# Linear attention and a gated FFN on one core: the first FFN product of two pairs of groups as seven half products, and numerators finished in PSUM

## The chip, the cores and the metric

The kernel runs on one core of a Trainium2 chip. The metric is device time in microseconds (us), from start to end of one execution; lower is better. Before the change three runs gave 367.69, 367.46 and 368.05 us, median 367.69. PE is the matrix engine, DVE the vector engine, ACT the scalar engine, POOL the GpSimd engine, SP the engine that issues most transfers. PE writes to PSUM, which has eight banks of 128 x 512 fp32; ACT and DVE read it.

## The reference

The inputs are q, k, v of (8 batches, 8 heads, 576 tokens, 64) and the weights. What is computed, cut from the reference:

```
def phi(x):
    proj = np.einsum('bhsd,df->bhsf', x, w_phi)
    proj = proj - np.max(np.abs(proj), axis=-1, keepdims=True)
    return np.concatenate([np.exp(proj), np.exp(-proj)], axis=-1)
q_p, k_p = (phi(q), phi(k))
kv = np.einsum('bhsf,bhsd->bhfd', k_p, v)
z = np.sum(k_p, axis=2)
num = np.einsum('bhsf,bhfd->bhsd', q_p, kv)
den = np.einsum('bhsf,bhf->bhs', q_p, z)[..., None] + 1e-06
...
x = (num / den).transpose(0, 2, 1, 3).reshape(4608, 512)
gate = np.maximum(x @ w_gate, 0.0)      # 512 -> 1536
val = x @ w_val                         # 512 -> 1536
return (gate * val @ w_out)             # 1536 -> 512
```

## The kernel before

**Units of work.** A batch has 512 tokens in four tiles of 128, and 64 left over. The leftovers of all eight batches make one more group of 512 tokens. So the FFN has nine groups: 0 to 7 for the batches and 8 for the leftovers (its steps carry the number of batches, 8; its tile is `xTm`, the others' are `xTs`). All of it is written as small steps, functions `do_xx`. The string `ORDER` lists some 2200 words such as `fv.3.7:5`, which is step `fv` for group 3, block 7, in PSUM bank 5; `@val2` gives a buffer. The words are recorded one after the other, and each engine does its own instructions in that order. So `ORDER` alone decides what an engine does next, in which bank and in which buffer. Groups run staggered: attention of batch b+1 lies between FFN steps of group b.

**Attention of one tile of 128 tokens.** `nu` (L904) multiplies the two feature halves (s = 0 and 1, from exp and exp of the negative) of a query tile `qp` with `kv`, for two or three heads in one bank, 65 columns for each head and s: 64 numerators and a denominator. Three `nu` cover eight heads. `nt` (L925) on DVE multiplies the s = 1 part with a scale `cq` into a buffer `t`; `nv` (L935) adds the s = 0 part into `u`; `nr` (L943) takes one reciprocal of eight denominators into `r`; and `nx` (L947) on POOL multiplies `u` with `r` into `xu` (bf16). `xt` transposes `xu` by DMA into `xT`, 512 features on partitions and 512 tokens along a row. `mn` (L1060) is `nu` for the leftover group.

**The FFN of a group.** For each of 12 blocks of 128 hidden features `fv` and `fg` (both through L1081) make `val` and `gate`: four matmuls of 128 x 128 weights on 512 tokens, one for each quarter of the 512 features. `va` (L1096, ACT) or `vb` (L1099, DVE) copies `val` to SBUF, and `ga` (L1102, DVE) makes `h = max(gate, 0) * val`. Group 0 does the same in quarter pieces (`pv`, `pg`, L1110).

**The second product** of groups 1 to 8 is already done with seven products of half size in place of eight: `fw` (L1247), each 12 matmuls of 256 columns. It needs four sums over halves of `h` for six blocks, `ps` on POOL or `ds` on DVE (both L1223), and sums of `w_out` made once, `tw` (L1203). Two of the sums write over `h` in place. The seven results are put together in SBUF: `ys` and `y2` copy on ACT (L1272, L1275), `yw`, `yz`, `y1`, `y3` and `y4` add on DVE (L1278). `ow` sends rows out.

**Filler.** `zz` (L442) multiplies zeros, 85 matmuls in the first part of the program.

Of the kernel before, what the change touches and what calls it, by code (L numbers as in the profile page):

```python
# [28 lines left out]
vd.0.0.0:2@vs1 qz.0.0:3@my1 vs.0.1.1 qe.0.1.1.1:5 vp.0:2 qu.0.1@mz0 ke.0.2.1.0:6 qe.0.1.1.0:5 wl.0.0
vz.0:2 qb.0.2:4 zz.2:7 qb.1.3:3 zz.2:7 qb.1.2:1 vd.0.0.1:2 qu.0.0@mz1 vz.1:2 qe.0.1.3.0:3@qp2  # L30
vo.2@vs2 qw.0.0@cq0 qx.0.0.3:0 qx.0.0.2:4 qe.0.0.0.0:2 vs.0.2.1 zz.7:7 kv.0.0:6 qx.0.1.3:3 lw.1.1
vs.0.2.0 kc.0.0:6@kv0 kt.1.1@kT3 qe.0.0.0.1:2 kv.0.2:5 kv.0.1:6 qe.0.0.2.1:4@qp3 lm.1.1 kc.0.2:5
wl.1.1 kc.0.1:6 nu.0.0.0:2 nt.0.0.0:2@t0 zz.1:7 nu.0.0.2:5 qw.0.1 qx.0.1.2:1 qe.0.0.2.0:4
qe.0.1.3.1:3 nu.0.0.1:6 nv.0.0.0:2@u0 zz.2:7 nu.0.1.2:4 lv.1.2 nu.0.1.0:2 qe.0.1.2.1:1 nt.0.0.1:6@t1
lm.1.0 nt.0.0.2:5@t2 qy.0.2:3 nv.0.0.1:6 qe.0.0.3.0:0 nv.0.0.2:5 nt.0.1.0:2@t3 zz.2:7 nu.0.1.1:6
qy.0.3:5 nr.0.0@r0 qe.0.1.2.0:1 qz.0.2:3@my2 nv.0.1.0:2@u1 qz.0.3:5@my0 qu.0.2@mz2 zz.5:7
kr.1.1:3125 qe.0.0.3.1:0 nt.0.1.2:4@t0 nt.0.1.1:6@t1 qw.0.2 wl.1.0 nu.0.2.2:0 nx.0.0@xu0 nv.0.1.2:4
xp.0.0:7 nv.0.1.1:6 nt.0.2.2:0@t2 ke.1.1.3.1:5@kp3 nr.0.1@r1 nu.0.2.1:4 xa.0.0:7 nt.0.2.1:4@t3
nu.0.2.0:6 ke.1.1.0.1:3 nt.0.2.0:6@t0 qu.0.3@mz1 ke.1.1.0.0:3 pv.1.0:7 nv.0.2.1:4@u2 nv.0.2.2:0
nv.0.2.0:6 nu.0.3.1:4 qw.0.3 ke.1.1.1.0:1 nx.0.1@xu1 kx.1.1.0:3@mk3 xp.0.1:0 pa.1.0:7@val0  # L40
# [12 lines left out]
qe.1.0.3.1:4 qe.1.0.2.1:7 vs.1.1.0 qx.1.0.3:4 qe.1.0.0.0:0 qe.1.0.0.1:0 fv.0.10:1 va.0.9:6@val0 wo.0
vq.1.0 kr.1.2:5046 vq.1.1 pb.0.3:2 qx.1.0.2:7 kx.1.2.0:5@mk5 qe.1.0.1.1:3 va.0.10:1@val3
qe.1.0.1.0:3 qe.1.0.2.0:7 kv.1.1:2 mt.0 wo.1 kx.1.2.3:6 qy.1.0:1 kc.1.1:2@kv1 fg.0.9:3
ke.1.2.0.0:5@kp0 qz.1.0:1@my1 kx.1.2.1:0 kx.1.2.2:4 ke.1.2.3.1:6 ku.2@kT3 vo.1.0@vs1 ke.1.2.1.1:0
kk.1.2.0@ek4 qu.1.0@mz0 vs.1.0.1 kk.1.2.1 ke.1.2.3.0:6 fv.0.8:7 ga.0.9:3 ke.1.2.0.1:5 fg.0.10:2
# [216 lines left out]
def kernel(  # L274
# [679 lines left out]
    def do_nx(bk, b, i):  # L954
        normalize(nc.gpsimd, b, i)
# [408 lines left out]
```

## Time and profile before

| | |
|---|---|
| median of the runs shown (lowest to highest) | 367.69 us (367.46 to 368.05) |
| the profiled execution: first to last instruction, which is the time that the profile gives for it | 365.2 us |
| difference between the two | 2.5 us |
| mean granted PE clock | 0.997 |
| matmuls, and weight loads | 3900 each |
| transfers: bytes, mean rate | 38.14 MB, 104 GB/s |

The profile is of one execution. Its page has the busy time of each engine as a share of the span, the chain of work that ended last, followed back from the end, and groups of instructions by source line with the mean time of one. A matmul's end is modelled, so that one of 512 columns is listed with 379 ns, though the next one starts sooner; how closely matmuls follow each other is read from pieces of the chain, which give a start, a length and a count. Windows give the busy time of each engine in a stretch of the span.

### The profile page before, as it was taken

The page shows a single profiled execution, that of the slowest core. Times are in us where ns is not written, and L with a number is a line of the kernel's source. Part 1 is how long each engine was busy: PE and PEld are TensorE (multiplying, and loading weights), DVE is VectorE, ACT ScalarE, POOL GpSimd, SP SyncE. Part 2 cuts the span into 40 slices and gives each one's busy share as a digit, 9 for nine tenths or more (in the row PEclk, how much of TensorE's full clock was granted, in tenths as well). Part 3 has the DMA queues.
Part 4 walks back from the last instruction along what each step waited for, and adds up shares of the span by engine and source line. Part 5 has one row for each costly group of instructions (what it writes and reads, how often), then busy time and mean ns, then how long its engine had stood idle before and what let it go on. Part 6 is the DMA issues. An engine that isn't in the chain of part 4 may idle for free.

```text
span 365.2 us, 10031 instructions
## 1 busy us (share of the span) xinstructions
PE 356.6 (98%) x3900; PEld 224.4 (61%) x3900; DVE 308.1 (84%) x723; ACT 228.8 (63%) x550; POOL 275.8 (76%) x337
## 2 busy tenths in 40 slices
PE   8999999999999999999999999999999999999993
PEld 6579865445575647755676456755457765545682
DVE  5999999989999998989988989899676945448872
ACT  4999996986698768695975278748854221121200
POOL 8765988999999999968997589946975793016600
PEclk9999999999999999999999999999999999999998
DMA  8999999983746893298219660397000320203016
GB/s 128 254 205 206 176 196 143 181 132 53 131 96 131 103 156 71 58 149 109 61 63 126 130 130 0 61 177 137 0 16 2 131 45 0 72 3 115 2 33 197
DMA packets 90768, 38.14 MB, mean 104 GB/s; under 512 B 64226, under 2 KB 86370, under 8 KB 90722
## 3 DMA queue, kind: packets, MB, share of 16 engines
q0 software_dynamic: 33504, 15.03, 32.5%
q1 hardware_dynamic: 56754, 21.83, 27.7%
q10 hardware_dynamic: 464, 0.66, 0.8%
q8 instruction: 30, 0.49, 0.6%
q14 instruction: 16, 0.13, 0.1%
HBM read 37.81 MB, written 9.44 MB: 129 GB/s over the span
## 4 chain that ended last, share of the span: by engine, by line
PE 81%; DVE 9%; POOL 4%; issue 2%; DMA 1%; ACT 1%; SPq 0%; DVEq 0%; POOLq 0%
PE bank L1081 42%; PE bank L1247 18%; PE bank L781 4%; PE bank L1110 4%; PE bank L904 3%; PE bank L1142 2%; PE bank L841 2%; PE bank L579 2%; POOL vs L1223 2%; DVE t L925 1%; DVE h L1102 1%; DVE u L935 1%; DMA w64f<-in_w_phi_dram 1%; ACT kp L675 1%; PE bank L442 1%
## 5 line engine op out<-in xcount | busy, mean ns | idle before, releaser
L675 ACT ACTIVATE kp<-bank 128x384 bf16<-128x384 f32 x192 | 84.1, 513 | 12.8 <-PE bank L579 6.0
L1081 PE MATMUL bank<-xTs,wv 128*128 128x512 bf16 x352 | 87.3, 379 | 0.0
L1096 ACT CAST val<-bank 128x512 bf16<-128x512 f32 x81 | 47.4, 592 | 62.8 <-PE bank L1081 55.7
L1081 PE MATMUL bank<-xTs,wg 128*128 128x512 bf16 x352 | 86.4, 379 | 0.0
L1102 DVE SCALAR_TENSOR_TENSOR h<-bank,val 128x512 bf16<-128x512 f32 x88 | 59.0, 681 | 22.1 <-PE bank L1081 15.0
L856 ACT ACTIVATE qp<-bank 128x512 bf16<-128x512 f32 x128 | 69.8, 619 | 5.3 <-PE bank L841 2.6
L1081 PEld LDWEIGHTS <-wg 128*128 128x128 bf16 x400 | 37.2, 98 | 41.0 <-issue 2.2
L1081 PEld LDWEIGHTS <-wv 128*128 128x128 bf16 x400 | 37.1, 98 | 38.0 <-DMA xTs<-xu 0.4
L732 POOL TENSOR_TENSOR vs<-vn,ek 128x780 bf16<-128x780 f32 (+2 forms) x40 | 53.9, 1364 | 1.2 <-ACT ek L692 0.7
L947 POOL TENSOR_TENSOR xu<-u,r 128x512 bf16<-128x512 f32 x36 | 37.3, 1044 | 16.8 <-DVE r L943 16.6
L683 DVE TENSOR_REDUCE mk<-bank 128x3 f32<-128x384 f32 x96 | 49.1, 542 | 1.0 <-ACT kp L675 0.9
L1247 PEld LDWEIGHTS <-h 128*128 128x128 bf16 x420 | 39.9, 98 | 9.5 <-issue 2.4
L1223 POOL TENSOR_TENSOR vs<-h 128x256 bf16<-128x256 bf16 x42 | 28.0, 670 | 21.4 <-DVE h L1102 14.4
L864 DVE TRANSPOSE_TENSOR_REDUCE maxq<-bank 128x16 f32<-128x512 f32 x56 | 37.1, 691 | 0.4 <-PE bank L841 0.2
L935 DVE TENSOR_TENSOR u<-bank,t 128x195 f32<-128x195 f32 (+1 forms) x108 | 32.7, 327 | 0.7
L925 DVE TENSOR_TENSOR t<-bank,cq 128x195 f32<-128x195 f32 (+1 forms) x96 | 29.4, 325 | 2.0 <-PE bank L904 1.7
L1247 PE MATMUL bank<-wo,h 128*128 128x256 bf16 x252 | 31.0, 273 | 0.0
L904 PEld LDWEIGHTS <-qp 128*128 128x128 bf16 x512 | 23.2, 98 | 10.8 <-issue 1.2
L1223 POOL TENSOR_TENSOR vs<-vs,h 128x256 bf16<-128x256 bf16 x42 | 27.9, 673 | 1.0 <-PE bank L1247 0.2
L904 PE MATMUL bank<-kv,qp 128*128 128x65 bf16 x512 | 26.1, 193 | 0.4 <-DVE u L935 0.2
L1223 POOL TENSOR_TENSOR h<-h 128x256 bf16<-128x256 bf16 x36 | 23.7, 670 | 0.3
L1223 POOL TENSOR_TENSOR h<-h,vs 128x256 bf16<-128x256 bf16 x36 | 23.7, 671 | 0.0
(134 smaller groups left out, 577.3 us busy)
## 6 DMA issues: line engine op xcount, KB each, us to landing
vn<-in_v_dram SPq DMA_DIRECT2D x24, 256.0 KB, 5.5
out_dram<-xTs SPq DMA_DIRECT2D x17, 256.0 KB, 2.4
kn<-in_k_dram POOLq DMA_DIRECT2D x7, 512.0 KB, 8.6
qn<-in_q_dram POOLq DMA_DIRECT2D x7, 512.0 KB, 8.0
out_dram<-obp SPq DMA_DIRECT2D x14, 256.0 KB, 2.4
wv<-in_moe_w_val_dram POOLq DMA_DIRECT2D x3, 512.0 KB, 8.9
wg<-in_moe_w_gate_dram POOLq DMA_DIRECT2D x3, 512.0 KB, 9.3
wo<-in_moe_w_out_dram POOLq DMA_DIRECT2D x3, 512.0 KB, 8.2
```

Of the source, the lines that this page charges most:

```text
L675: nc.scalar.activation(kp_of(3 * b + j)[:, i, s].rearrange("p n f -> p (n f)"), bank[bk[0]][:, 0 : 3 * F], AF.Exp, scale=(1.0, -1.0)[s],)
L683: nc.vector.tensor_reduce(mk_of(3 * b + j)[:, :, i], bank[bk[0]][:, 0 : 3 * F].rearrange("p (n f) -> p n f", f=F), axis=AX.X, op=ALU.max, ...
L732: nc.gpsimd.tensor_tensor(vs_of(3 * b + j)[:, s, 0:n].rearrange("p n i e -> p (n i) e")[:, :, 0:e], src[:, lo:hi].rearrange("p h i e -> p ...
L856: nc.scalar.activation(qp_of(4 * b + i)[:, s, 4 * hq : 4 * hq + 4].rearrange("p h m -> p (h m)"), bank[bk[0]], AF.Exp, scale=(1.0, -1.0)[s],)
L864: nc.vector.tensor_reduce((maxq0[:, i] if b == 0 else maxq)[:, :, i, 4 * hq : 4 * hq + 4].rearrange("p t h -> p h t"), bank[bk[0]].rearran ...
L904: nc.tensor.matmul(bank[bk[0]][:, E * n : E * (n + 1)], lhsT=qp_of(4 * b + i)[:, s, h, :], rhs=kv_of(b)[:, h, s, 0:E],)
L947: eng.tensor_tensor(xu_of(n).rearrange("p (h d) -> p h d", d=D), u_of(n)[:, :, 0:D], r_of(n).to_broadcast([P, H, D]), op=ALU.mult,)
L1081: nc.tensor.matmul(bank[bk[0]], lhsT=w[:, dc, P * f : P * f + P], rhs=xT(g)[:, dc, :], start=(dc == 0), stop=(dc == NDC - 1),)
L1096: nc.scalar.copy(val_of(NFC * g + f), bank[bk[0]])
L1102: nc.vector.scalar_tensor_tensor(h2_of(g, f), bank[bk[0]], 0.0, val_of(NFC * g + f), op0=ALU.max, op1=ALU.mult)
L1223: eng.tensor_tensor(sum_of(g, n, j), a, b, op=op)
L1247: nc.tensor.matmul(bank[bk[0]][:, col : col + HN], lhsT=x[:, P * u : P * (u + 1)], rhs=w, start=(n in (1, 5, 6) and u == us[0] and j == 0) ...
```

## The change

There are four parts, and a new `ORDER` over all of them (2386 words).

**Pairs.** Groups 5 and 6, and 8 and 7, are each taken as a pair. For a block of 128 hidden features the four results (gate and val of two groups) were 4 x 4 matmuls. They become seven half products `fi` with two matmuls each, 14 in place of 16, of sums and differences of the groups' `xT` and of the weights. `x` sums (`xs` on POOL, `xd` on DVE) are 16 in all, weight sums (`wt` on POOL, `wu` on DVE) 24, each of 128 x 512 bf16. One of the weight sums is written over `wv`. The results are gathered in PSUM: `ia` and `ib` on ACT copy a bank to another bank, where the next half product adds to it; product 5 goes to SBUF once (`iq` on ACT, `ir` on DVE), and `iv` on DVE adds it to a bank for each of the two `val`. `ga` is as before. Steps `fv`, `fg`, `va` and `vb` remain for groups 1 to 4.

**Seeds in the second product.** `fa` and `fb` copy a bank to a bank on ACT, and `fw` adds on top, so that the adds on DVE are `y1` and `y4` alone, with one copy each (`yq` or `zq`, `y2` or `z2`, `y3` or `z3`) beside them.

**Numerators in PSUM.** `nu` is split by s and takes four heads: s = 1 is multiplied into a bank, `nt` scales it in place, s = 0 is added on top by PE, and `nr` and `nx`, both on DVE, read the bank. `nv` and the buffers `t` and `u` are gone.

**Sums on POOL.** The 24 sums `ds` on DVE become `ps` on POOL.

How often each step stands in `ORDER`, where that differs:

```
fv 100 -> 52   fg 100 -> 52   fi 0 -> 168   va 81 -> 48   vb 19 -> 4
ia 0 -> 24     ib 0 -> 24     iq 0 -> 19    ir 0 -> 5     iv 0 -> 48
wt 0 -> 18     wu 0 -> 6      xs 0 -> 11    xd 0 -> 5     ds 24 -> 0     ps 168 -> 192
nu 96 -> 128   mn 12 -> 16    nt 108 -> 72  nv 108 -> 0   nr 36 -> 72    nx 36 -> 72
fa 0 -> 8      fb 0 -> 9      ys 8 -> 0     yw 8 -> 0     yz 8 -> 0      fw 58 -> 57
y1 9 -> 8      y2 8 -> 5      y3 8 -> 7     y4 9 -> 9     yq 0 -> 3      zq 0 -> 5
z2 0 -> 3      z3 0 -> 1      kc 20 -> 23   kd 4 -> 1     xa 3 -> 4      xc 1 -> 0
```

The diff, cut to its core (of `ORDER` one line):

```diff
-fg.1.1:6 ps.1.2.2 lv.3.1 nr.2.1@r2 fv.1.7:4 ps.1.1.4 ke.3.0.2.0:2 ps.1.3.4 ke.3.0.2.1:2 ps.1.1.5
+iv.1.10.0:7@val3 ps.6.2.3 ps.7.1.1 ps.7.1.0 ps.7.3.1 y3.5:3 fi.1.10.2:0 fw.6.1:6 fi.1.10.7:2
...
-    def do_nu(bk, b, i, g):
-        lo, hi = GROUPS[g]
+    HALVES = ((0, 4), (4, 8))
+    def do_nu(bk, b, i, g, s):
+        lo, hi = HALVES[g]
         for h in range(lo, hi):
-            for s in range(2):
-                n = 2 * (h - lo) + s
-                nc.tensor.matmul(
...
+            n = h - lo
+            nc.tensor.matmul(
+                bank[bk[0]][:, E * n : E * (n + 1)],
+                lhsT=qp_of(4 * b + i)[:, s, h, :],
+                rhs=kv_of(b)[:, h, s, 0:E],
+                start=(s == 1 and h == lo),
+                stop=(h == hi - 1),
+                skip_group_check=(s == 0),
+            )
...
     def do_nt(bk, b, i, g):
         nc.vector.tensor_tensor(
-            t_of(3 * serial(b, i) + g)[:, 0:n],
-            parts(bk, n)[:, :, 1],
+            part(bk, g),
+            part(bk, g),
             scales(b, i)[:, lo:hi][:, :, None].to_broadcast(...),
             op=ALU.mult,
         )
-    def do_nv(bk, b, i, g):
...
+    def do_nr(bk, b, i, g):
+        nc.vector.reciprocal(r_of(serial(b, i))[:, lo:hi], part(bk, g)[:, :, D : D + 1])
-    def do_nx(bk, b, i):
-        normalize(nc.gpsimd, b, i)
+    def do_nx(bk, b, i, g):
+        nc.vector.tensor_tensor(
+            xu_of(n).rearrange("p (h d) -> p h d", d=D)[:, lo:hi],
+            part(bk, g)[:, :, 0:D],
+            r_of(n)[:, lo:hi].to_broadcast([P, hi - lo, D]),
+            op=ALU.mult,
+        )
...
+    PAIRS = ((5, 6), (8, 7))
+    def weight_sum(eng, n, dc, third):
+        a, b = {
+            1: lambda: (at(wv_sb, dc), at(wg_sb, dc)),
+            2: lambda: (at(wv_sb, 2 + dc), at(w_sum(1), dc)),
+            3: lambda: (at(wv_sb, 2 + dc), at(wv_sb, dc)),
+            4: lambda: (at(wg_sb, 2 + dc), at(w_sum(2), dc)),
+        }[n]()
+        eng.tensor_tensor(at(w_sum(n), dc), a, b, op=ALU.subtract)
+    def token_sum(eng, p, n, dc):
+        a, b, op = {
+            1: lambda: (x_part(p, 3), x_part(p, 4), ALU.add),
+            2: lambda: (x_sum(p, 1), x_part(p, 1), ALU.subtract),
+            3: lambda: (x_part(p, 1), x_part(p, 3), ALU.subtract),
+            4: lambda: (x_part(p, 2), x_sum(p, 2), ALU.subtract),
+        }[n]()
+    def do_fi(bk, p, f, n):
...
+        for dc in range(2):
+            nc.tensor.matmul(
+                bank[bk[0]],
+                lhsT=w[:, dc, P * f : P * f + P],
+                rhs=x[:, dc, :],
+                start=(n in (1, 5) and dc == 0),
+                stop=(dc == 1),
+                skip_group_check=(n not in (1, 5)),
+            )
+    def do_ia(bk, p, f):
+        nc.scalar.copy(bank[bk[1]], bank[bk[0]])
+    def do_ib(bk, p, f):
+        nc.scalar.copy(bank[bk[1]], bank[bk[0]])
+    def do_iq(bk, p, f):
+        nc.scalar.copy(qs_of(("in", p, f)), bank[bk[0]])
+    def do_iv(bk, p, f, u):
+        nc.vector.tensor_tensor(
+            val_of(NFC * PAIRS[p][u] + f), bank[bk[0]], qs_of(("in", p, f)), op=ALU.add
+        )
...
-                    start=(n in (1, 5, 6) and u == us[0] and j == 0),
+                    start=(n in (1, 5) and u == us[0] and j == 0),
...
+    def do_fa(bk, g):
+        nc.scalar.copy(bank[bk[1]], bank[bk[0]])
```

Two places of the order show the shape of it. On DVE, the numerators of tiles of batch 7, before (`t` and `u` are the buffers of scaled part and sum, `cq` the scale, `obp` and `xTs` output rows of the second product):

```order
L925 TENSOR_TENSOR t_124<-bank_66,cq_116 128x130
L1278 TENSOR_TENSOR xTs<-bank_69,xTs 128x2x256
L1102 SCALAR_TENSOR_TENSOR h_152<-bank_64,val_141 128x512
L925 TENSOR_TENSOR t_123<-bank_63,cq_116 128x130
L925 TENSOR_TENSOR t_126<-bank_65,cq_116 128x195
L925 TENSOR_TENSOR t_125<-bank_68,cq_116 128x195
L935 TENSOR_TENSOR u_129<-bank_63,t_123 128x130
```

The same batch on DVE after the change (`r` holds reciprocals, `xu` normalised tokens, `qs` the copied product 5 of the pair, `qp_114` and `h_148` blocks of `h`):

```order
L948 TENSOR_TENSOR bank_70<-bank_70,cq_116 128x260
L1100 SCALAR_TENSOR_TENSOR qp_114<-bank_67,val_136 128x512
L1201 TENSOR_TENSOR val_134<-bank_66,qs_140 128x512
L1201 TENSOR_TENSOR val_137<-bank_68,qs_140 128x512
L957 RECIPROCAL r_125<-bank_70 128x4
L961 TENSOR_TENSOR xu_126<-bank_70,r_125 128x256
L948 TENSOR_TENSOR bank_66<-bank_66,cq_116 128x260
L1100 SCALAR_TENSOR_TENSOR h_148<-bank_64,val_134 128x512
L957 RECIPROCAL r_125<-bank_66 128x4
```

One bank is now scaled in place and later read twice, and the attention of batch 7 stands among the blocks of the pair (5, 6) rather than behind group 6.

On ACT, late in the program, before: what it does for groups 7 and 8 is to copy `val` to SBUF and, for the second product, a bank to `obp`, `xTm` or `xTs`.

```order
L1096 CAST val_143<-bank_66 128x512
L1096 CAST val_144<-bank_70 128x512
L1096 CAST val_142<-bank_66 128x512
L1272 COPY obp<-bank_63 128x2x256
L1096 CAST val_142<-bank_66 128x512
L1096 CAST val_144<-bank_65 128x512
L1275 COPY xTm<-bank_63 128x2x256
```

And after, at the first blocks of the pair (5, 6), where `COPY bank<-bank` is `ia` (L1189) or `ib` (L1192) and `qs` takes product 5:

```order
L1380 COPY obp<-bank_67 128x2x256
L1189 COPY bank_67<-bank_65 128x512
L1195 COPY qs_139<-bank_63 128x512
L1195 COPY qs_140<-bank_64 128x512
L1192 COPY bank_64<-bank_67 128x512
L1195 COPY qs_138<-bank_63 128x512
L1189 COPY bank_63<-bank_66 128x512
L1192 COPY bank_64<-bank_63 128x512
```

A copy to SBUF that only DVE waited for has become a copy between banks that PE waits for.

701 lines of the change are left out of this document (378 added, 323 removed).

## The prediction, made before the run

> **What bounds the kernel now.** I read the page's busy shares first, then the busy time by stretch, then the end of the chain, then what PE waits for. The shares:
>
> ```profile
> PE 356.6 (98%) x3900; PEld 224.4 (61%) x3900; DVE 308.1 (84%) x723; ACT 228.8 (63%) x550; POOL 275.8 (76%) x337
> ```
>
> A modelled matmul end makes PE look busier than it is, so 98% proves nothing alone. By stretch (columns: start and end, length, then busy time of PE, of weight loads, DVE, ACT, POOL, the granted clock, DMA share, GB/s):
>
> ```profile
> 0.00:75.00 75.00, 72.66 (x1006) 49.83 (x1007) 70.56 (x179) 65.42 (x167) 61.97 (x73) 1.00 1.25 188
> 75.00:150.00 75.00, 74.71 (x892) 46.21 (x891) 71.52 (x171) 58.36 (x143) 74.16 (x88) 1.00 0.61 103
> 150.00:225.00 75.00, 74.99 (x831) 44.46 (x830) 69.17 (x162) 51.88 (x124) 62.47 (x78) 1.00 0.60 97
> 225.00:285.00 60.00, 59.99 (x655) 36.83 (x656) 47.72 (x105) 39.94 (x96) 45.66 (x56) 1.00 0.38 61
> 285.00:342.00 57.00, 57.00 (x365) 31.88 (x364) 35.24 (x80) 11.44 (x21) 26.25 (x38) 1.00 0.18 57
> 342.00:365.20 23.20, 17.23 (x157) 15.17 (x155) 13.93 (x30) 1.76 (x3) 5.29 (x8) 0.95 0.33 91
> ```
>
> PE has 2.34 us without work in the first 75 and 0.29 in the next, then almost none until the last stretch. Beside it DVE is nearly full to 225 (70.56, 71.52 and 69.17 of 75) and POOL is full from 75 to 150 (74.16). Later DVE has room: 47.72 of 60 and 35.24 of 57. The chain decides who is followed. Its shares by engine, and its last pieces but some short ones (start, length, what):
>
> ```profile
> PE 81%; DVE 9%; POOL 4%; issue 2%; DMA 1%; ACT 1%; SPq 0%; DVEq 0%; POOLq 0%
> ...
> 316.71 13.81 PE bank L1081 x64
> 330.53 1.31 PE bank L1247 x12
> 331.84 10.36 PE bank L1081 x48
> 342.20 17.05 PE bank L1247 x156
> ...
> 359.26 0.42 DVE xTs L1278
> ```
>
> 64 matmuls of 512 columns take 13.81 us and 48 take 10.36: 216 ns from one to the next in both, and each piece begins where the one before ends, up to 359.25. There PE's matmuls are the time. Only 9% of the chain is DVE and 4% POOL. Last, all that PE waits for by name (in total, times, longest):
>
> ```profile
> PE bank L442 <- DVE zero L428: 1.1, 1, 1.1
> PE bank L655 <- DVE w L418: 0.5, 1, 0.5
> PE bank L1110 <- ACT xTs L998: 0.2, 1, 0.2
> PE bank L904 <- DVE u L935: 0.2, 1, 0.2
> PE bank L904 <- ACT kv L792: 0.2, 1, 0.2
> PE bank L1247 <- DVE obp L1278: 0.2, 1, 0.2
> ```
>
> The first two are the start of the program. All later ones sum to 0.8 us; shorter waits hide under the modelled ends. PE is bound by its own stream from 150 on, and PE and DVE are bound together before.
>
> **PE, the half products.** 96 calls of `fv` and `fg` go, 384 matmuls; 168 `fi` with two each come, 336. That is 48 matmuls fewer, of the same shape and weights' size: the quoted piece x48, 10.36 us. Where they lie (this line's instructions alone: PE and weight loads, clock, DMA):
>
> ```profile
> 0.00:210.00 210.00, 93.94 (x397) 35.95 (x398) 1.00 0.85 133
> ```
>
> 397 of the 800 run before 210, so the 384 of groups 5 to 8 come behind it, where PE has no idle time that could hide the gain. `nu` and `mn` keep their matmuls (512 and 128) and only come in other groups; `fw` keeps 672. Nothing is added to PE's stream: a matmul that adds onto a seeded bank is the same matmul. Term: -10.4.
>
> **DVE, step by step.** The rows, by shape:
>
> ```profile
> L935 DVE TENSOR_TENSOR u<-bank,t 128x195 f32<-128x195 f32 x72 | 24.3, 352 | 0.7
> L925 DVE TENSOR_TENSOR t<-bank,cq 128x195 f32<-128x195 f32 x64 | 21.4, 345 | 1.3 <-PE bank L904 1.1
> L1278 DVE TENSOR_TENSOR obp<-bank,obp 128x512 f32<-128x512 f32 x21 | 14.2, 681 | 4.3 <-PE bank L1247 4.3
> L1099 DVE CAST val<-bank 128x512 bf16<-128x512 f32 x19 | 13.0, 682 | 4.3 <-PE bank L1081 4.3
> L935 DVE TENSOR_TENSOR u<-bank,t 128x130 f32<-128x130 f32 x36 | 10.0, 278 | 0.1
> L943 DVE RECIPROCAL r<-u 128x8 f32<-128x8 f32 x36 | 6.6, 189 | 0.2
> L1278 DVE TENSOR_TENSOR xTs<-bank,xTs 128x256 f32<-128x256 f32 x4 | 1.7, 424 | 0.3 <-PE bank L1247 0.2
> L1223 DVE TENSOR_TENSOR h<-h,vs 128x256 bf16<-128x256 bf16 x6 | 3.1, 525 | 0.0
> L1223 DVE TENSOR_TENSOR kp<-kp,vs 128x256 bf16<-128x256 bf16 x6 | 1.6, 281 | 0.0
> ```
>
> Numerators: before, each of 36 tiles has a 130-column and two 195-column pairs of `nt` and `nv` and one reciprocal: 2 x (0.28 + 2 x 0.35) + 0.19 = 2.15 us. After, two `nt` of 260 columns (between 0.35 at 195 and 0.68 at 512, so 0.42), two reciprocals of at most 0.19, two `nx` of 256 columns (0.42): 2.06. That is -3. No row shows DVE writing to PSUM; if it costs as little more or less as 0.06 us a time (ACT's rows below differ so), 72 of them are 4 us either way; I take none. `iv`, 48 x 0.68 = 32.7, and `ir`, 5 x 0.68 = 3.4, come. 15 `vb` go (-10.2), 24 `ds` go (half at about 0.52, the others from 0.28 up, 0.35 on average, -10.4). Of the second product's 42 adds (38 x 0.68 + 4 x 0.42 = 27.5) 26 adds and copies stay, two of them halves: 24 x 0.68 + 2 x 0.42 = 17.2, so -10.3. Three copies of `kv` and one of `xT` go to ACT, -2. Eleven sums `wu` and `xd` of 512 bf16 come: twice 0.28 at the least, twice 0.525 at the most, 0.7 taken, 7.7. The Trainium skill's page SBUF — State Buffer, section Who interferes with whom, says that a DVE instruction with two SBUF inputs and a POOL instruction reading SBUF exclude each other; the trace's 0.525 beside POOL's sums against 0.28 agrees, and by that rule each of the eleven could wait out one of POOL's 1.16 us sums, 13 us in place of 7.7. In sum DVE gets +7.9: 308 to 316, of some 357.
>
> **ACT and POOL.** The rows:
>
> ```profile
> L1096 ACT CAST val<-bank 128x512 bf16<-128x512 f32 x81 | 47.4, 592 | 62.8 <-PE bank L1081 55.7 <-DVE h L1102 5.2 <-DVE u L935 0.6
> L692 ACT ACTIVATE ek<-mk 128x12 f32<-128x12 f32 x46 | 9.9, 240 | 0.1
> L703 ACT ACTIVATE bank<-mk 128x12 f32<-128x12 f32 x2 | 0.4, 180 | 0.0
> L947 POOL TENSOR_TENSOR xu<-u,r 128x512 bf16<-128x512 f32 x36 | 37.3, 1044 | 16.8 <-DVE r L943 16.6
> L1223 POOL TENSOR_TENSOR vs<-h 128x256 bf16<-128x256 bf16 x42 | 28.0, 670 | 21.4 <-DVE h L1102 14.4 <-PE bank L781 5.3 <-DMA xTm<-xu 1.5
> L1203 POOL TENSOR_TENSOR kp<-wo 128x768 bf16<-128x768 bf16 x4 | 6.6, 1647 | 0.0
> ```
>
> ACT: 33 `va` go, 84 copies `ia`, `ib`, `iq`, `fa`, `fb` come, five small changes: about 52 x 0.59 = 31 us more, 229 to 260. A copy into a bank may be 0.06 shorter than one to SBUF (180 against 240 ns for 12 elements). ACT has 62.8 us of idle time before `va` alone, so these lie beside PE. POOL: 36 `nx` go (-37.3), 24 `ps` come (16.1), and 29 sums of 512 columns (midway between 0.67 at 256 and 1.65 at 768: 1.16, so 33.6): 276 to 288. It is relieved where it was full, 75 to 150, and loaded where it had room, from about 220. Behind the new sums stand `ps` of groups 5 to 8, for which `fw` waits. All transfers stay the same in number; `xt` of batch 7 stands earlier on SP, ahead of pair (8, 7), and the DMA share is 0.38 and 0.18 there. Pair (8, 7) then waits for `xt`, and for up to eight token sums behind it (five of 0.7, three of 1.16 us, on two engines); the rest of pair (5, 6) and `fw` of group 5 stand beside it on PE.
>
> **New waits.** This is the unknown term. PE now waits for another engine to write back into PSUM before it adds: 64 `nu` and 8 `mn` after `nt`, 48 `fi` after `ia` or `ib`, 17 `fw` after `fa` or `fb`: 137 places. What is queued behind such a wait is all of PE. Upper end: 0.2 us each, the length of the later waits above, is 27 us. Lower end: below nothing, since the new order may close the old 0.8 us, some of the 2.6 us idle in the first 150, and no more: -2. Between them I go by how full DVE is. Its spare time falls from 57 to about 41 us over the program, so most of it becomes like the first 150 us, where DVE was busy 142 of 150 and PE lost 2.6 us. I take that, +2.5. The end of the program, 17 us of `fw`, then an add and a transfer, keeps its shape: 0.
>
> **The sum.** 365.2 - 10.4 + 2.5 = 357.3 for the span; the median lies 2.5 us above the profiled span: **359.8 us**.
>
> **The rivals.** *PE waits on the write-backs.* If the 137 places cost more than 10.36 / 137 = 76 ns each on average, the change is slower. A bank has to go through a copy of 0.59 us or a DVE step of 0.42 behind whatever is queued there, and eight banks must serve more partial results at once. At 0.1 us each: 367.7 - 10.4 + 13.7 = 371.0. For it: ACT and DVE stand in one PE queue's way 137 times more. Against it: the later waits sum to 0.8 us now, though the kernel already reuses banks after every `nt` and `nv`. Chance 0.10.
>
> *DVE takes over the second half.* From 225 to 342 DVE has 47.72 + 35.24 = 83 us of work. To it come 32.7 + 3.4 + 7.7 = 43.8 us, and of the 30.9 that go (`ds`, `vb`, adds) I estimate two thirds here, 20.6: 106 us in a stretch that PE would leave in 117 - 10.4 = 106.6. If DVE can be filled no further than from 150 to 225 (69.17 of 75, 92%), the stretch takes 115.2 and the gain is 1.8: 365.9. For it: DVE is on 9% of the chain already. Against it: the order takes batch 7's attention forward, so the load is spread. Chance 0.14, with the time from 363.5 to 368.
>
> *DVE is the limit all through.* Then the time follows DVE's total, +7.9: 375.6. The quoted gapless 13.81 and 10.36 us pieces, with DVE at 35.24 of 57 beside them, speak against it. Chance 0.04. The Trainium skill's Perfetto Trace Analysis, section Identifying the Most-Contended Engine, would have it so: it calls matmul busy time a bad measure, takes weight loads' busy share for PE, which is 61% here, and names the engine of highest occupancy, which is then DVE with 84%. The pieces of the chain disagree with that ranking.
>
> *The order closes old gaps too.* With the lower end of the waits: 367.7 - 10.4 - 2 = 355.3. POOL's relief between 75 and 150 speaks for it. Chance 0.06.
>
> **How the numbers follow.** The forecast, 359.8 with 355.5 to 363.5 of its own, has the remaining 0.66. The range of 355.0 to 367.5 leaves out the two slower cases (0.14), and about half of the fastest case and a little of DVE's second half (0.05 together). A measurement of this kernel can tell about 0.2%, 0.7 us, from no change. Faster: the forecast, the fastest case, and 0.08 of the 0.14 of DVE's half, 0.80. Same: 0.05 of it. Slower: 0.01 of it, and the two slower cases, 0.15.
>
> **What would show it.** Right: matmuls of the first product fall from 800 to 752 in pieces of 216 ns each; PE's idle time stays within a few us; PE's waits on ACT's copies and on `nt` sum to some 2 us; DVE about 316, ACT 260, POOL 288. Wrong: `fi`, `nu` or `fw` waiting 10 us or more in all; DVE full from 200 on with PE idle beside it; `iv`, `nt` or bank copies much longer than the rows used; PE idle at the start of pair (8, 7), behind `xt` and its sums.

## The result, and the profile after

| | before | after |
|---|---|---|
| median of 4 runs | 367.86 us (367.46 to 368.05) | 385.90 us (382.70 to 390.81) |
| ratio of the two | | 1.0462, interval 1.0415 to 1.0509 |
| predicted | | 359.8 us (355.0 to 367.5) |
| profiled run: its time, its span | 367.7, 365.2 us | 390.81, 388.8 us |

The kernel is slower by 17 us (by the ratio; 18 by the medians) where 8 us of gain were forecast, and it lies outside the range. The profiled run is the slowest of the four, and the ratio leaves it out as a slow one: its mean granted clock is 0.965, in the others 0.973 to 0.982, and below it is seen where the clock drops. The page of after, its shares and two rows of the 40 slices (each 9.72 us):

```profile
PE 357.8 (92%) x3852; PEld 225.2 (58%) x3852; DVE 329.4 (85%) x692; ACT 254.5 (65%) x604; POOL 287.4 (74%) x354
...
PE   8878999999969999997999999349999999999996
...
PEclk9998999999988999998999999859999999999999
```

PE was 8.6 us without work before (365.2 - 356.6); now it is 31.0. Its busy time is 1.2 us longer though 48 matmuls fewer run. 22.4 + 1.2 make the 23.6 us by which the span grew. The row of PE shows three notches, at slices 12, 19 and 26 to 27, and the granted clock drops at each or just behind it. By stretch (start and end, length, then PE, weight loads, DVE, ACT, POOL, clock, DMA share, GB/s):

```profile
0.00:75.00 75.00, 68.04 (x974) 49.24 (x975) 65.41 (x160) 61.52 (x156) 44.56 (x55) 0.98 1.03 158
105.00:120.00 15.00, 11.24 (x73) 5.64 (x75) 9.36 (x19) 8.16 (x18) 11.27 (x13) 0.77 0.90 118
170.00:190.00 20.00, 18.02 (x179) 10.83 (x177) 16.11 (x37) 13.95 (x34) 12.90 (x16) 0.91 0.50 100
240.00:270.00 30.00, 18.71 (x254) 14.15 (x253) 27.71 (x42) 16.31 (x40) 20.21 (x23) 0.77 0.19 45
285.00:345.00 60.00, 59.08 (x334) 30.72 (x333) 51.98 (x88) 26.20 (x49) 39.49 (x54) 1.00 0.10 27
```

240 to 270 alone loses 11.3 us of PE, 0 to 75 loses 7.0 (before 2.3), 105 to 120 3.8 and 170 to 190 2.0. In 285 to 345, where two thirds of the half products run (228 of 336), only 0.9 is missing. What PE waits for in after (in total, times, longest), the longest first:

```profile
PE bank L1052 <- DVE bank L948: 11.4, 2, 11.3
PE bank L1079 <- DMA xTs<-xu: 3.5, 1, 3.5
PE bank L924 <- DVE bank L948: 2.0, 1, 2.0
PE bank L802 <- POOL vs L753: 1.8, 2, 1.1
```

One wait of 11.3 us: `mn` (L1052) for `nt` (L948). It stands at one of the 137 write-back places of the prediction. But `nt` isn't long. DVE's timeline there (start, length, operation, the last number how many):

```profile
244.40 0.72 DVE L961 TENSOR_TENSOR xu<-bank,r 128x256 bf16<-128x256 f32 x2
245.04 12.08 DVE L1124 TENSOR_TENSOR vn<-wv,wg 128x512 bf16<-128x512 bf16 x1
257.04 0.76 DVE L948 TENSOR_TENSOR bank<-bank,cm 128x260 f32<-128x260 f32 x2
```

The row of 12.08 us is `wu.1.0.0`, the first of the eleven sums that DVE was given; the other ten took 6.8 us together, one of them, on the same tiles at 272.78, 0.40. The two `nt` behind it take 0.76. POOL in the same microseconds, the first and the last row of its run:

```profile
244.31 1.29 POOL L1322 TENSOR_TENSOR vs<-vs,h 128x256 bf16<-128x256 bf16 x2
...
253.47 3.37 POOL L1151 TENSOR_TENSOR qT<-xTs 128x512 bf16<-128x512 bf16 x3
```

From 245.04 on POOL works through 14 operations on SBUF without a gap, two of them 1.50 us and none longer, until 256.84; DVE's sum ends at 257.12, 0.28 us later. DVE is reported busy for 12.08 us over a sum that takes 0.40 elsewhere, and gets through only when POOL's run is over: this is called shut out below. The chain of waits can't say so (start, length, what):

```profile
245.04 0.49 DVE vn L1124
245.53 11.51 issue
```

"issue" is time in which the engine waited for nothing that the profile shows. The row became readable only with POOL's timeline beside it.

The clock follows. Cut at steps of 3.41 us (columns as above):

```profile
245.99:249.40 3.41, 0.61 (x21) 0.59 (x17) 3.41 (x1) 1.83 (x4) 3.41 (x7) 1.00 0.70 83
249.40:252.81 3.41, 0.00 (x0) 0.00 (x0) 3.41 (x1) 0.00 (x0) 3.41 (x4) 0.50 0.56 186
...
256.23:259.64 3.41, 1.79 (x22) 1.40 (x22) 3.37 (x9) 1.19 (x3) 0.61 (x1) 0.50 0.00 0
259.64:263.05 3.41, 3.41 (x21) 1.61 (x19) 2.13 (x5) 1.65 (x4) 0.68 (x1) 0.50 0.00 0
263.05:266.47 3.42, 3.42 (x33) 3.06 (x32) 2.83 (x5) 3.42 (x8) 2.69 (x3) 1.00 0.00 0
```

The first row still has full speed; after it the windows run at half speed, and full speed is back only behind one in which PE was busy throughout. PE's 5.2 us of work (1.79 + 3.41) between 256.23 and 263.05 would have taken half of that, so this gap costs 2.6 us more than it lasts. The other three pieces at half speed (30.94 to 34.36, 112.86 to 119.69, 177.72 to 181.13) cost some 6.2 by the same reckoning, an estimate from the windows' busy times. Ahead of these three PE had been busy 2.31, 1.15 and 1.43 of 3.41 us. The Trainium skill, "TensorE: Matmul & The Clock Gate", Part 1 on the clock gate, states a free-running window of 3413 ns and half speed after an idle one; the grid agrees, but here a window with PE busy 0.61 of 3.41 us was enough.

### The profile page after: what moved, and what is told of

It is laid out like the page before. It is cut to its first block, busy times and chain, and to the rows that moved or that the text cites. A ratio compares the mean times of both kernels' runs of the same rounds, so it can differ in the third digit from the quotient of the medians.

```text
span 388.8 us, 10030 instructions
## 1 busy us (share of the span) xinstructions
PE 357.8 (92%) x3852; PEld 225.2 (58%) x3852; DVE 329.4 (85%) x692; ACT 254.5 (65%) x604; POOL 287.4 (74%) x354
## 4 chain that ended last, share of the span: by engine, by line
PE 59%; DMA 13%; POOL 9%; DVE 8%; issue 7%; ACT 2%; SPq 0%; DVEq 0%; POOLq 0%
PE bank L1346 18%; PE bank L1079 15%; PE bank L1179 14%; DMA qn<-in_q_dram 4%; PE bank L924 3%; DMA xTs<-xu 3%; DMA vn<-in_v_dram 2%; PE bank L802 2%; POOL vs L753 2%; DMA wo<-in_moe_w_out_dram 2%; DMA vm<-in_v_dram 2%; PE bank L862 2%; PE bank L1241 1%; PE bank L600 1%; DVE h L1100 1%
## 5 line engine op out<-in xcount | busy, mean ns | idle before, releaser
L1079 PE MATMUL bank<-xTs,wv 128*128 128x512 bf16 x208 | 53.8, 391 | 4.1 <-DMA xTs<-xu 3.5
L1079 PE MATMUL bank<-xTs,wg 128*128 128x512 bf16 x208 | 52.0, 379 | 0.4 <-DVE h L1100 0.2
L885 DVE TRANSPOSE_TENSOR_REDUCE maxq<-bank 128x16 f32<-128x512 f32 x56 | 36.6, 683 | 7.5 <-PE bank L862 7.5
L1322 POOL TENSOR_TENSOR vs<-h 128x256 bf16<-128x256 bf16 x36 | 23.9, 667 | 21.8 <-DVE h L1100 21.8
L1094 ACT CAST val<-bank 128x512 bf16<-128x512 f32 x48 | 28.7, 612 | 14.3 <-PE bank L1079 11.6
L1201 DVE TENSOR_TENSOR val<-bank,qs 128x512 bf16<-128x512 f32 x48 | 31.8, 684 | 7.5 <-PE bank L1179 6.8
L1079 PEld LDWEIGHTS <-wv 128*128 128x128 bf16 x208 | 18.7, 99 | 24.6 <-issue 7.7
L1079 PEld LDWEIGHTS <-wg 128*128 128x128 bf16 x208 | 18.4, 97 | 21.4 <-issue 3.2
L1192 ACT COPY bank<-bank 128x512 f32<-128x512 f32 x24 | 13.6, 571 | 23.8 <-PE bank L1179 15.2
L961 DVE TENSOR_TENSOR xu<-bank,r 128x256 bf16<-128x256 f32 x72 | 28.5, 410 | 0.9 <-DMA xTs<-xu 0.4
L948 DVE TENSOR_TENSOR bank<-bank,cq 128x260 f32<-128x260 f32 x64 | 25.5, 429 | 2.0 <-PE bank L924 1.3
L1189 ACT COPY bank<-bank 128x512 f32<-128x512 f32 x24 | 13.6, 572 | 17.3 <-PE bank L1179 9.0
```

What stands on the lines that cost most here:

```text
L885: nc.vector.tensor_reduce((maxq0[:, i] if b == 0 else maxq)[:, :, i, 4 * hq : 4 * hq + 4].rearrange("p t h -> p h t"), bank[bk[0]].rearran ...
L1079: nc.tensor.matmul(bank[bk[0]], lhsT=w[:, dc, P * f : P * f + P], rhs=xT(g)[:, dc, :], start=(dc == 0), stop=(dc == NDC - 1),)
L1201: nc.vector.tensor_tensor(val_of(NFC * PAIRS[p][u] + f), bank[bk[0]], qs_of(("in", p, f)), op=ALU.add)
L1322: eng.tensor_tensor(sum_of(g, n, j), a, b, op=op)
```

## The experiments

Three theories stood after this trace. *The shut-out*: the one sum costs the 11 us and its half clock, whatever the write-backs do. *All eleven*: each DVE sum loses something to POOL, so all should go. *The order*: the table's new sequence is late in many places, and the sum is only where it shows. In all its runs before took between 366.6 and 368.4 us. In e5, e6 and e7 the order stands on one line, so their line numbers are 274 lower (L805 for L1079, L687 for L961, L588 for L862).

### All eleven sums on POOL, or only one

```diff
# e1: every wu.* -> wt.*, every xd.* -> xs.*
# e2: this one alone
-wu.1.0.0
+wt.1.0.0
```

> The eleven weight sums and half differences that the change moved to DVE (all `wu` and `xd`) go back to POOL; all else is the change. Theory A (a DVE sum with both inputs in SBUF was shut out while POOL ran its own sums back to back, 12.08 us for one row; PE idled 11.26 us behind it and then ran at half clock, which cost 2.6 us more): the row's 12 us, PE's 11.26 us gap at 246 us and the half clock behind it are gone, 13 us less than the changed kernel, so 371 to 374 us, still slower than before (367.9). Rival B (the long row was a wait of another kind, or at most one POOL sum's 1.16 us): the gap only moves, 384 to 390 us. Rival C (the loss is spread over the 137 new waits on write-backs and over late DMA landings): under 4 us less, 382 to 387 us. POOL gets about 11 x 1.16 = 13 us more work, busy near 300 us.

> Only the one sum that took 12.08 us (`wu.1.0.0`) goes back to POOL; the other ten stay on DVE. Theory A: nearly the whole gain of the eleven, 371 to 375 us, since the other ten took 0.4 to 1.2 us each; DVE's busy time falls from 329 by about 12 to 317 us. Rival B: within 2 us of the changed kernel (384 to 388 us). A third way: another of the ten meets the next burst in its place, and one row of 5 us or more shows up elsewhere; then 378 to 388 us.

Measured: e1 381.12 us (380.33 to 382.76), ratio 1.0373 (1.0345 to 1.0401). e2 374.81 (373.00 to 376.47), ratio 1.0195 (1.0153 to 1.0237). e2 lies where the shut-out had put it; e1 doesn't (371 to 374 was expected). One word of the order is worth 11.1 us against the median of after, 10.0 against the middle one of its three other runs (384.85); the other ten moved as well cost 6.3. The shares and longest waits of e2:

```profile
PE 350.9 (95%) x3852; PEld 222.0 (60%) x3852; DVE 317.8 (86%) x691; ACT 254.2 (68%) x604; POOL 289.2 (78%) x355
```

```profile
PE bank L1079 <- DMA xTs<-xu: 2.8, 2, 2.6
PE bank L802 <- POOL vs L753: 1.9, 2, 1.2
PE bank L1179 <- POOL kp L1124: 1.9, 3, 0.9
```

The 11.3 us wait is gone and nothing as long has taken its place; DVE's total falls from 329.4 to 317.8. In e1 PE waits for POOL instead:

```profile
PE bank L1346 <- POOL h L1322: 3.1, 4, 1.8
...
PE bank L1179 <- POOL qr L1151: 1.4, 1, 1.4
PE bank L1346 <- POOL vs L1322: 1.3, 2, 1.1
```

So the other ten sums stood better on DVE, and "all eleven" falls.

### The fourth part of the change alone, on the kernel before

```diff
-ds.
+ps.
```

> The kernel before with the fourth part of the change alone: the eight sums `ds` on POOL in place of DVE. It takes about 8 x 0.5 us off DVE and puts 8 x 1.16 us on POOL. My forecast priced this at nothing on the path: 367.9 within 1 us. If POOL's sums shut DVE out wherever the two meet (theory A in a strong form), the kernel before slows as well: 370 us or more, with a DVE row of over 3 us.

(The edit turns all 24 of the kernel's `ds`, not eight.) Measured: 371.70 us (370.78 to 372.60), ratio 1.0119 (1.0099 to 1.0140): 4.0 us slower, with nothing else changed. What PE waits for in e3, first row:

```profile
PE bank L1247 <- POOL vs L1223: 2.6, 2, 1.4
```

Both waits lie between 349 and 353 us, in the program's last stage. DVE has no sum of two SBUF inputs left there, so this isn't the shut-out: POOL is late with sums that `fw` needs. The prediction had cost this part at nothing on PE's path. In after the order around it is another, so the 4.0 can't be carried over as it stands.

### What shuts DVE out

e4 is a small program of its own: DVE meets runs of POOL's sums.

> A kernel of its own, which leaves the whole computation out and writes zeros: one DVE operation on 128x512 bf16 meets a run of POOL sums. Theory A: a DVE sum with two SBUF inputs, 0.39 us by itself, lasts until POOL's run ends, so its time grows with the run: 4, 8 and 16 POOL sums of 256 columns (about 0.6 us each) give about 2.5, 5 and 10 us, 8 sums of 512 columns about 9 us; a DVE sum with one input in PSUM is not held (under 1 us); in the run where POOL waits for ScalarE between its sums, DVE gets in at the first pause (under 1.5 us). Rival B: at most one POOL sum's time is added, so 0.4 to 1.6 us whatever the run's length. Open, with no forecast: a DVE copy with one SBUF input against POOL sums, and a DVE sum against POOL copies with one SBUF input.

DVE's one operation in each stretch (busy us, then mean ns):

```profile
L69 DVE TENSOR_TENSOR r_wide<-src 128x512 bf16<-128x512 bf16 x1 | 1.2, 1247 | 0.0
...
L69 DVE TENSOR_TENSOR r_sixteen<-src 128x512 bf16<-128x512 bf16 x1 | 0.8, 764 | 0.0
L71 DVE TENSOR_TENSOR r_bank<-bank,src 128x512 bf16<-128x512 f32 x1 | 0.7, 680 | 0.0
```

Alone the sum took 414 ns. Beside a run of four POOL sums of 256 columns it took 762, beside sixteen 764, beside sums of 512 columns 1247; with one input in PSUM 680, the usual time of such a row. Here DVE waits out one POOL sum, however many follow. The Trainium skill, "SBUF — State Buffer", Who interferes with whom, states this lock, and e4 agrees. Nothing of 12 us comes out of it. So the place was tried: the sum later (e7) and earlier (e13) in DVE's row, and another third of the weights, so other inputs and another output (e11), in after with no other edit.

```diff
# e7
-wu.1.0.0 mn.2.1.1:6
+mn.2.1.1:6
...
+nt.8.2.0:0 wu.1.0.0
# e11
-wu.1.0.0
+wu.1.0.2
...
-wt.1.0.2
+wt.1.0.0
# e13
+wu.1.0.0 nr.6.0.0:6
```

> The changed kernel (385.9 us) with the sum that took 12.08 us, `wu.1.0.0`, still on DVE, but in the order behind the two numerator sums `nt.8.2.1` and `nt.8.2.0` for which PE waited 11.26 us. Theory A (POOL's run of sums keeps this DVE sum out, and what stands behind it on DVE pays): a long row is still there or not, but PE's 11.26 us gap and the half clock behind it are gone: 372 to 378 us. If something else than its place on DVE held PE, the gap stays: 384 to 388 us. As to the row itself: if POOL's run always shuts a sum out, it lasts until POOL pauses again, 5 us or more; if the 12.08 us came of one particular meeting, it takes 0.4 to 1.3 us here as the ten other sums did.

> The changed kernel (385.9 us) with two sums exchanged: where DVE did `wu.1.0.0` (columns 0 to 511) it does `wu.1.0.2` (columns 1024 to 1535), and POOL does the first in place of the other, 8 words later. Same engines, same place, same kind and size. If the place in time and POOL's run decide, the long row is there again, over 10 us, and the time is 382 to 388 us; if these very columns decide (their places in SBUF, who else uses them), the row takes 0.4 to 1.3 us and the time is 372 to 377 us, as with the sum on POOL.

> The changed kernel (385.9 us) with `wu.1.0.0` on DVE some 1 to 2 us earlier: ahead of the reciprocals and products that release the transpose of `xu` at 244.8 us, in the middle of the same run of POOL's sums. If the transpose's issue decides: the row takes 0.4 to 1.3 us and the time is 372 to 378 us. If POOL's run at this place decides: a row of 11 us or more again, 383 to 388 us.

Measured: e7 384.85 us (382.68 to 387.34), e11 386.19 (382.52 to 392.37), e13 379.53 (377.84 to 380.73). The sum's row in DVE's timeline, in e7, e11 and e13:

```profile
242.27 11.48 DVE L850 TENSOR_TENSOR vn<-wv,wg 128x512 bf16<-128x512 bf16 x1
```

```profile
242.51 12.08 DVE L1124 TENSOR_TENSOR vn<-wv,wg 128x512 bf16<-128x512 bf16 x1
```

```profile
239.20 6.25 DVE L1124 TENSOR_TENSOR vn<-wv,wg 128x512 bf16<-128x512 bf16 x1
```

All three are shut out again, and each ends 0.28 or 0.29 us after POOL's gapless run does; in e13 that run is shorter, because POOL has to wait for ACT's `ek` at 245.2. ACT in turn waits 6.35 us for a `mk` that stands behind the sum on DVE, so there the shut-out ended because it left POOL without work. With the shorter row e13, and e14 below, lie between the two times that were expected of each. In e7 PE's longest wait moves to other matmuls and stays as long:

```profile
PE bank L588 <- DVE xu L687: 10.5, 1, 10.5
```

The place by a few words and the third of the weights are ruled out. Three more programs of their own looked for the trigger: 42 sums at stepped times against POOL's operations (e8), 64 with all tiles at the kernel's places in SBUF and a wait on POOL (e9), 64 beside a transpose, a plain copy or nothing on SP (e12).

> A kernel of its own, which leaves the whole computation out and writes zeros: POOL runs the 14 operations that it ran from 244.3 to 256.8 us in the changed kernel, in the same sizes and kinds, and a DVE sum meets them at 14 starting points about 25 ns apart, alone in the first 14 passes and twice in a row in the last 14. If being shut out hangs on the moment at which DVE asks, some of the 28 passes show a sum of 5 us or more; if POOL's kinds of operation matter (the short runs of equal sums gave 0.77 to 1.25 us), all do; if it needs something else of the changed kernel, all sums take 0.4 to 1.3 us.

> A kernel of its own, which leaves the computation out and writes zeros: as the one before it (28 meetings, none over 0.81 us), but with the changed kernel's tiles at the changed kernel's places in SBUF, a wait on POOL at the sum as there (long over when the sum starts), and DVE asking in the second to third of POOL's 14 operations, at 32 points 17 ns apart; the first 32 passes do the sum that was shut out (`wv` less `wg` into `vn`), the last 32 another weight sum (`wv` less `vn` into `kp`'s place). If the places or the wait make the difference, the first 32 show sums of 5 us or more and the others do not; if the moment does, some of both; if it takes more of the changed kernel (its PE, ScalarE or DMA at work), none, all 0.4 to 1.3 us.

> A kernel of its own, which leaves the computation out and writes zeros: as the last one of that kind, but DVE first writes `xu` from PSUM, as in the changed kernel, and in passes 1 to 32 SP then issues a transpose of `xu` while the sum asks for its turn, in passes 33 to 48 a plain copy, in the last 16 nothing. If the transposes' issue is what lets POOL keep DVE out, the sums of the first 32 passes last 5 us or more and the last 16 at most 1.3 us (the copies tell whether any issue on SP does it). If it is not, all last 0.4 to 1.3 us.

The sums of e12, in ns the shortest, the median and the longest:

```profile
L108 DVE TENSOR_TENSOR vn<-wv,wg x64: 441/566/758, 56.5 to 917.2; 128x512 bf16<-128x512 bf16 x64
```

e8 gave 0.41 to 0.80 us and e9 0.41 to 0.94. None of 170 sums was shut out beyond one POOL operation. In these programs PE's work, the bulk loads and nearly all of ACT's are left out; whether these matter wasn't tried. Back in the kernel, on the best version found by then (e10, below, where POOL does this sum): a spare sum of the same inputs on DVE at that place without any wait (e15), the same just ahead of the next DVE sum (e16), the real sum on DVE into the spare tile with ACT copying it on (e17), and e15 with a wait on POOL (e18). e14 is e10 with the sum on DVE at e13's place.

```diff
# e15
+    nc.vector.tensor_tensor(spare, wv_sb[:, 0, 0:SF], wg_sb[:, 0, 0:SF], op=ALU.subtract)
-wt.1.0.0
+wt.1.0.0 wu.9.0.0
# e16
+wu.9.0.0 wu.2.1.0@kp1
# e17: step wu.8 copies the result to its place, and wt.1.0.0 goes
+    nc.scalar.copy(w_sum(1)[:, 0, 0:SF], spare)
+wu.9.0.0 wu.8.0.0
# e18: as e15, and POOL writes 32 columns of spare before
```

> The kernel of e10_qn_late (369.7 us: loads of V late, load of Q late) with `wu.1.0.0` back on DVE at the earlier place of e13_sum_earlier, which takes 1.14 us off POOL where PE waits for POOL's sums (1.51 and 0.52 us at 242 us). If the sum is let in there: 367 to 369.5 us, level with the kernel before; if it is shut out there too: 378 us or more.

> The kernel of e10_qn_late (369.7 us, the sum on POOL) with one more DVE sum, `wv` less `wg` into a spare tile that nobody reads, at the place in DVE's order at which the changed kernel's sum was shut out. It waits for nothing and nothing waits for it, only DVE's next operations stand behind it. If POOL's run shuts such a sum out at this place, the row lasts 5 us or more and the kernel takes 376 to 384 us; if the long row was a hidden wait of the real sum or came of its destination `vn`, the row takes 0.4 to 1.3 us and the time is 368 to 372 us.

> The same, with the spare sum just ahead of `wu.2.1.0`, a sum that was let in after 0.73 us in the middle of the same run of POOL's. If the inputs `wv` and `wg` decide, it is shut out here as well, 5 us or more; if the moment in the program decides, both take 0.4 to 1.3 us and the time is 368 to 372 us.

> The kernel of e10_qn_late (369.7 us) with the sum back on DVE at the place where it was shut out, but into the spare tile, without a wait on POOL; ScalarE copies it to `vn` (0.6 us of its time). If destination or wait were the cause, the sum takes 0.4 to 1.3 us, POOL is 1.14 us less busy where PE waits for it (1.51 and 0.52 us at 242 us), and the time is 367 to 370 us. If POOL's run shuts it out all the same: 376 to 384 us.

> The kernel of e15_spare_here (the spare sum where the real one was shut out, let in after 1.25 us) with one thing more: POOL writes 32 columns of the spare tile shortly before, so that the spare sum carries a wait on POOL's semaphore that is met long before it starts, as the real sum does. If the wait is what makes the difference, the row lasts 5 us or more and the kernel takes 376 to 384 us; if it is the destination `vn`, the row takes 0.4 to 1.3 us as in e15, 368 to 372 us.

| | e14 | e15 | e16 | e17 | e18 |
|---|---|---|---|---|---|
| time, us | 377.09 (4 runs) | 368.60 (1) | 372.46 (1) | 379.96 (4) | 379.37 (1) |
| the sum's row, us | 6.25 | 1.25 | 0.62 | 12.07 | 13.37 |

The spare sum of e15 and the sum of e17 in DVE's timelines:

```profile
233.25 1.25 DVE L1130 TENSOR_TENSOR spare<-wv,wg 128x512 bf16<-128x512 bf16 x1
```

```profile
233.76 12.07 DVE L1130 TENSOR_TENSOR spare<-wv,wg 128x512 bf16<-128x512 bf16 x1
```

e17 has no wait ahead of its sum and is shut out, so the wait isn't the cause, though e15 and e18 taken alone would say so. Nor is the moment against POOL's operation: the sums of e13, e14 and e15 all start 0.18 us after POOL began the same 512-column sum, and only e15's is let in when that ends. Nor is it the inputs alone: e16's sum reads the same ones in the same run of POOL's and takes 0.62 us. Eight profiles have a DVE sum at this place, and in seven it waits out POOL's whole run. What decides it stays open.

### The order's own losses

The new order starts late at the head. In e2, without the shut-out, the first two stretches:

```profile
0.00:75.00 75.00, 67.04 (x973) 48.69 (x974) 64.85 (x159) 61.29 (x155) 44.25 (x55) 0.98 1.05 159
75.00:150.00 75.00, 70.69 (x795) 40.46 (x794) 68.02 (x152) 61.20 (x153) 65.66 (x72) 1.00 0.85 125
```

PE loses 12.3 us there, before 2.6, and POOL does 44.25 us of work in the first 75 where it did 61.97. Of three edits of the transfers on e2, e5 issues two V loads of group 1 later (near 23 us in place of 5.2 and 5.9, as in before), e6 a Q load earlier, and e10 is e5 with that Q load later.

```diff
# e5: both lv from further ahead
+lw.1.1 lv.1.2 lv.1.1
# e6: lq.4.2 from behind vs.3.0.1
+lq.4.2 lm.4.1
# e10, on e5
+ps.1.1.4 lq.4.2
+kt.4.0@kT3 qt.4.0@qT2
```

> The kernel with one sum moved to POOL (374.8 us), and in its order two words of SP's queue moved: the loads of V for group 1 (`lv.1.2`, `lv.1.1`, 256 KB each, issued at 5.2 and 5.9 us) stand behind `lw.1.1` and so go out near 23 us, as in the kernel before. Theory D (part of the loss lies in the new order's landings: in the head these loads share the DMA engines with group 0's Q, K and V, the V load issued at 6.97 us lands after 9.92 us and POOL's first sum starts at 17.03 us, in the kernel before 13.44): POOL's first sum starts 2 to 3.5 us earlier, the half clock at 23.5 us (1.45 us) goes, and the time falls by 2 to 5 us, to 370 to 373. Rival: the head's loss is POOL's and ACT's work, not the loads: within 1 us of 374.8.

> The kernel with one sum moved to POOL (374.8 us), and in its order one word of POOL's queue moved: the 512 KB load of Q `lq.4.2`, issued at 103.65 us, stands ahead of `lm.4.1` and goes out near 98 us. Theory D: the transpose of `xu` issued at 106.67 us lands 6.62 us later because that load is under way beside it; with the load over by then it lands in 3 to 4 us, PE's gap of 2.59 us at 110.8 us shrinks below 0.5, and the time falls by 2 to 3 us, to 372 to 373. Rival: the transposes ahead of it are slowed in turn and the gap moves to 104 us: within 1 us of 374.8.

> The kernel with one sum on POOL and the two loads of V late (372.6 us), and the 512 KB load of Q `lq.4.2` now later instead of earlier: behind three sums and two others on POOL, so that it goes out near 109 us, after the transposes of `xu` issued at 100.5 to 106.7; the transposition on DVE that reads it (`qt.4.0`) moves with it. Theory D: the transposes land in 3 to 4 us in place of 6.6, PE's gap of 3.1 us at 108.6 us and the half clock behind it (2.88 us) go: 366 to 369 us, at or a little below the kernel before. Rival: the gap moves to where group 4 waits for its Q, some 6 us later: 371 to 375 us.

Measured: e5 372.56 us (372.38 to 374.17), ratio 1.0142 (1.0116 to 1.0168). e6 375.32 (374.74 to 376.35), no gain on e2. e10 369.65 (368.04 to 371.73, 10 runs), ratio 1.0063 (1.0040 to 1.0087). POOL's first scaled V block in e2 and in e5, with its wait in brackets:

```profile
17.03 1.47 POOL L753 TENSOR_TENSOR vs<-vn,ek 128x768 bf16<-128x768 f32 x1 [3.58 <-DMA vn<-in_v_dram]
```

```profile
14.09 1.47 POOL L479 TENSOR_TENSOR vs<-vn,ek 128x768 bf16<-128x768 f32 x1 [2.22 <-DMA vn<-in_v_dram]
```

The place of the two loads is worth 2.9 us to POOL there (before it started at 13.44), and 2.2 us to the medians, of which the intervals of e2 and e5 still overlap. For e10's further 2.9 the intervals of e5 and e10 are apart. In after that Q load stood beside the transposes for which PE waits 3.5 us (second row of its waits, above). The chain there:

```profile
100.56 4.00 DMA xTs<-xu
...
106.43 7.50 DMA xTs<-xu
...
114.07 2.29 PE bank L1079 x5
```

The second transpose takes 7.50 us. In e6 the load goes out at 101.80 in place of 103.65, still beside a transpose, issued at 102.17, which takes 7.63 us. The gap only moves, to a wait for DVE's `xu`, which stands behind that transpose:

```profile
PE bank L805 <- DVE xu L687: 3.7, 1, 3.7
```

In e10 the clock is 1.0 throughout, and PE's longest waits are these:

```profile
PE bank L1179 <- POOL kp L1124: 1.9, 3, 0.9
PE bank L463 <- ACT kp L696: 1.8, 2, 1.2
PE bank L1346 <- POOL h L1322: 1.7, 2, 1.3
```

No version beat the kernel before. e10's span of 367.4 is 2.2 us over before's, with 10.4 us of matmuls less and a shorter end (below, 2.6), so some 15 us are lost in many small waits. e10's trace lacks 47 matmul records, so they can't be shared out by stage there. e2's is complete: PE lacks 8.0, 4.3 and 0.8 us in the first three stretches of 75, 0.7 from 285 to 345, and 3.0 between, where DVE is busy 54.79 of 60:

```profile
225.00:285.00 60.00, 56.97 (x595) 32.87 (x588) 54.79 (x132) 40.42 (x92) 51.48 (x54) 1.00 0.32 73
```

Which waits make up these losses wasn't settled.

## Why the prediction was wrong

**The matmuls: right.** In 285 to 345 PE is busy 59.08 of 60 us, and the longest piece of PE in the chain of after shows the price, 219 ns each where 216 was taken:

```profile
318.56 10.52 PE bank L1179 x48
```

48 fewer such matmuls run, 752 for 800. The gain was made and given back elsewhere.

**The write-backs: not the loss.** In the whole of after PE's one named wait for an ACT copy into a bank is this:

```profile
PE bank L1179 <- ACT bank L1192: 0.2, 1, 0.2
```

`nt` in PSUM took 0.43 us (0.42 taken), `iv` 0.68. The rival in which 137 write-backs cost 0.1 us each falls: the waits of `mn` and `nu` are two of 11.3 and 2.0 us and little else, and the long one was caused by DVE's queue, not by the write-back.

**The totals: right.** ACT 254.5 (260 predicted), POOL 287.4 (288), DVE 317.8 in e2 (316), where the long row is gone. The two rivals in which DVE becomes the limit fall as the main cause. In 285 to 345 PE is busy 59.08 of 60 us beside a DVE with 51.98, and e2 is 10 us faster with the other ten sums still on DVE. From 225 to 285 DVE is 91% full in e2 and PE lacks 3.0 us, so that much of "DVE takes over the second half" isn't excluded.

**The failed step: new waits, +2.5.** It was drawn from how full DVE is: 2.5 us, where the profiled execution lost 36.6 (23.6 + 10.4 + 2.6) and the median 31.0 (18.0 + 10.4 + 2.6). Of these 31.0, 11.1 hang on one sum (e2) and 5.2 on the places of three loads (e5, e10), neither of which fullness shows; some 15 aren't assigned to single causes. In the part on DVE the sums stood at 0.7 us, at most one POOL sum of 1.16 each, and only as busy time. Two things were missed there. What stands behind a DVE sum, `nt` for `mn`, is PE's path, so a long row is a wait of PE. And the bound itself fails, 12.08 against 1.16. No row of before has such a thing: its 24 `ds` met POOL, and the longest took 0.78. One of the signs named as "wrong" did come, `mn` beside `nu` and `fw` with 10 us and more, but by a cause that no rival had.

**The transfers: costed at nothing, and wrong.** "All transfers stay the same in number" is true, and the 5.2 us hang on their places (e2 to e5 to e10; the first step, 2.2, lies within the scatter of the two). The prediction looked at `xt` of batch 7 only; the loss was at the head and at a Q load at 100 us, places of the order that it took as unchanged. Of the four parts, `ds` to `ps` costs before 4.0 us (e3), not nothing.

**The half clock: absent from the sum.** No row of before has PE idle for a window until its end. In the profiled execution of after it adds, by the estimate above, about 8.8 us (2.6 + 6.2) to gaps that were there for other reasons.

**The end: 0 predicted, 2.6 gained.** In before the last piece of PE ends at 359.25 and the span at 365.2; in after it ends 3.3 us before the span does.

```profile
383.32 2.14 PE bank L1346 x18
```

Why the last adds and transfers are shorter wasn't looked into.

## What to carry to other kernels

A change that removes work from a full engine has to be followed at the engines that now stand in its path: read what is queued behind each new instruction, on DVE above all, and treat a meeting of a two-input DVE operation with a long gapless run of POOL as a wait of unknown length, not as one POOL operation. When an order is written anew, list the landings of all transfers against the old order, since their number tells nothing. And a gap of PE of some microseconds costs more than it lasts where the clock drops behind it, here 2.6 us on top of 11.3.

## What was not expected of the hardware

A DVE sum with both inputs in SBUF waited out a POOL run of 14 operations, 12.08 us, and was released 0.28 us after its end; at this place of the program seven of eight profiles have such a row, 6.25 to 13.37 us long. In the eighth and in all other meetings seen (170 in small programs among them) it was let in after one POOL operation, 1.25 us at most. The chain of waits showed this as "issue". The clock's half speed came in whole pieces of a fixed grid of 3.41 us, also after windows in which PE had been busy, by the modelled ends, for up to 0.68 of the time (2.31 of 3.41).
